# Unequal token blocks, ten attention phases and a new prologue order in a gated-attention and two-layer MLP kernel

## The chip, the cores and the metric

One NeuronCore of a Trainium2 chip runs the whole program. The time is device microseconds of one execution; the kernel before was run three times, and its median is what the kernel after is held against.

## What is computed

A gated linear attention over 768 positions for 4 batches of 8 heads of width 48 gives 3072 tokens of 384 features. Two dense layers follow.

```python
for t in range(S):
    state = f[:, :, t, :, None] * state + np.einsum('bhd,bhe->bhde', k[:, :, t], v[:, :, t])
    y[:, :, t] = np.einsum('bhd,bhde->bhe', q[:, :, t], state)
...
a = x @ w_a          # x: (3072, 384), w_a and w_b: (384, 1536)
b = x @ w_b
x = (a * b) @ w_out  # (1536, 384)
...
h = x @ w_in         # (384, 2048)
out = (h - np.tanh(h)) @ w_out2
```

The inputs are float32 (weights arrive as 64-bit numbers, whose bits VectorE turns into float32). Every dense product is made as three matmuls, high part by high, high by low and low by high (`mm_split`, L163 to L165), each operand being split into two parts.

## The kernel before

The attention is cut into 24 steps (`attn_step`, L293), one for 64 positions of two batches, which give 128 tokens. A step is a generator; each `next` issues one phase. Its phases, by the letters that the change gives them: **F** the sigmoid of the gates (ACT, L303) and **P** the running product of the gates (DVE, L304); **R** the reverse scan (DVE, L307 to L312); **K** three products KH, RA and RB (DVE, L317 to L319); **S** the scores sc and the transposes pk on PE (L321 to L328) and **M** their masking and copies (ACT, and POOL for the steps under `PSEL`, DVE for the others, L329 to L339); **U** the state update uu (PE, then DVE or ACT, then POOL, L341 to L364); **Y** the output yy on PE (L366 to L374) and **E** its split into x high and low (ACT and DVE, L375 to L385); **D** DMAs that put rows of x in place (L387 to L393).

Six token blocks of four steps (512 tokens) go through layer 1 (`moe1`, L474). A block has 12 inner rounds m of three slots, one group of nine matmuls each: a, then b, then y of the round before (L452 to L454). So a block has 36 slots (`SLOTS`). One PSUM bank holds a and one holds b, so b of the next round waits until gf = a*b (DVE, L494) has been made, and y waits for gh and gl, the two parts of gf.

The first four steps are the prologue, whose order is written out by hand as a string (`SEQ`, L58): a digit issues the next phase of that step, f, t, v and w issue loads, x a dummy matmul on PE, c one weight conversion. The other 20 steps are spread over the slots by `OFF` (L55): a step takes nine slots, and its phases come at fixed slots in it, three slots early (`LEAD`). Block 0 thus carries the four steps that block 1 needs, and so on; the last block carries none.

The weights of layer 1 are 36 tiles. Each is converted by three DVE instructions (`w_start`, L125 to L127) and split by one ACT copy and one POOL subtraction (`w_finish`, L137 to L139). Four conversions are started in the prologue, and one in each slot of block 0 (L546). The 32 tiles of layer 2 are converted in blocks 1 to 4, two per nine slots (`CONV`), there with the subtraction on DVE as well, and stored to DRAM; the last block loads them back. Layer 2 then runs with 1728 matmuls of 512 columns.

Every engine works through its queue in the order in which the program issues, and so does SP with most of the DMAs.

Of the kernel before, what the change touches and what calls it, by code (L numbers as in the profile page):

```python
# [28 lines left out]
def tile_kernel(ctx: ExitStack, tc: tile.TileContext, q, k, v, f, w_a, w_b, w_out, w_in, w_out2, l_fkq, l_tv, l_v, l_w1, l_w2, out):  # L29
# [14 lines left out]
        w.bitcast(I32) for w in (w_a, w_b, w_out, w_in, w_out2, l_w1, l_w2))  # L44

    NSTEP = 2 * NC
    blocks = [4, 4, 4, 4, 4, 4]
    NBLK = len(blocks)
    first = [sum(blocks[:j]) for j in range(NBLK)]
    block_of = [j for j, n in enumerate(blocks) for _ in range(n)]  # L50
    PRO = blocks[0]
    SLOTS = 3 * MF
    STEP = SLOTS // 4
    LEAD = 3
    OFF = (0, 1, 3, 5, 7, 8, 9)  # L55
    CONV = (2, 6)
    PSEL = 2 * PRO
    SEQ = ("f0 f1 t0 t1 v0 f2 t2 v1 w f3 t3 w v2 w v3 w x x x x 0 0 x 1 0 x 0 1 x 1 x 1 2 x 0 2 0 x 2 2 1 x 1 3 3 x 3 c 3 2 "  # L58
           "x 2 c f4 t4 v4 3 x c 3 x 4 x 4 c")
    TW = 528  # L60

    const = ctx.enter_context(tc.tile_pool(name="const", bufs=1))
# [49 lines left out]
    def w_load(item):  # L112
        name, m = item
        st = stage.tile([128, 2 * DM], I32, tag="wst", name="wst", bufs=3)
        src = l_w1[m, :, "abo".index(name)] if name in "abo" else l_w2[m, :, "ip".index(name)]
        nc.sync.dma_start(out=st, in_=src)
        return name, m, st
# [12 lines left out]
    def w_finish(item):  # L130
        name, m, st, c = item
        if name in "abo":
            wt = wpool.tile([128, 2, DM], F32R, tag="w", name=f"w_{name}{m}")
            W[name, m] = (wt[:, 0], wt[:, 1])
        else:
            wt = st.bitcast(F32R).rearrange("p (h n) -> p h n", h=2)
        nc.scalar.activation(wt[:, 0], c, ACTF.Copy)  # L137
        eng = nc.gpsimd if name in "abo" else nc.vector
        eng.tensor_tensor(wt[:, 1], c, wt[:, 0].bitcast(F32), ALU.subtract)  # L139
        if name not in "abo":  # L140
            spilled.append((name, m, wt))
# [25 lines left out]
    with tc.manual_schedule(), ExitStack() as p1:  # L167
# [65 lines left out]
        def t_of(i):  # L233
            return T[i if i < min(PRO, 4) else i % 2]

        def tv_of(i):
            return TV[i if i < min(PRO, 4) else i % 2]

        def w_of(i):
            return work[i if i < PRO else 0]  # L240

        def load_t(i, sl):
            t = t_of(i)
            if i < PRO:
                nc.sync.dma_start(out=t[:, sl], in_=l_fkq[i, :, sl])
            else:
                for r0 in (0, 64):
                    nc.sync.dma_start(out=t[r0:r0 + D, sl], in_=l_fkq[i, r0:r0 + D, sl])

        def load_v(i):  # L250
            w = w_of(i)
            for ab, (vs, r0) in enumerate(((w.VS_A, 64), (w.VS_B, 0))):
                nc.sync.dma_start(out=vs[r0:r0 + 64], in_=l_v[i, ab])
            if i < PRO:
                load_tv(i)

        def load_tv(i):
            nc.sync.dma_start(out=tv_of(i), in_=l_tv[i])
# [29 lines left out]
        Y3 = {}  # L288

        def warm():  # L290
            nc.tensor.matmul(bank(7, "warm"), wdum[:, 0:128], wdum, start=True, stop=True)

        def attn_step(i):  # L293
            c, hb = divmod(i, 2)
            jb = block_of[i]
            si = i - first[jb]
# [29 lines left out]
            for j in range(NJ):  # L326
                nc.tensor.transpose(  # L327
                    pk[:, 128 * j:128 * (j + 1)], KH[:, 2 * j:2 * j + 2, :].rearrange("p u s -> p (u s)"), ident)  # L328
            for r_, rows in ((RA, slice(64, 128)), (RB, slice(0, 64))):  # L329
                if i < PSEL:  # L330
                    nc.scalar.activation(r_[rows], sc[rows], ACTF.Copy)
                    nc.gpsimd.affine_select(
                        out=r_[rows], in_=r_[rows], compare_op=ALU.is_ge, fill=0.0,
                        base=0, pattern=[[0, U], [1, CH]], channel_multiplier=-1,
                    )
                else:
                    m3 = mask.unsqueeze(1)
                    nc.vector.tensor_tensor(r_[rows], sc[rows], m3[rows].to_broadcast([64, U, CH]), ALU.mult)
# [29 lines left out]
            for u in range(U - 2 if direct else U):  # L368
                for r0, vs, rr, ab in ((0, VS_A, RA, 0), (64, VS_B, RB, 1)):
                    dst = yy[r0:r0 + 64, u]  # L370
                    nc.tensor.matmul(dst, vs[:, u], rr[:, u], start=True, stop=not direct)  # L371
                    if direct:
                        nc.tensor.matmul(dst, VX[i % 2][ab][:, u % 2, u // 2], rr[:, U - 2 + u % 2],
                                         start=False, stop=True)  # L374
            if si == 0:  # L375
                X[jb] = xp.tile([128, 2, KT, 4, 128], F32R, tag="x", name="x")
                if not direct:
                    Y3[jb] = xp.tile([128, 2, 4, 128], F32R, tag="y3", name="y3", bufs=1)
# [24 lines left out]
        def flag(pr):  # L403
            nc.tensor.transpose(pr[0:1, 0:128], ru, ident)
            nc.vector.tensor_reduce(r2, pr[0:1, 0:128], mybir.AxisListType.X, ALU.min)
            nc.vector.tensor_scalar(okf, r2, 0.5, None, ALU.is_ge)

        gens = {i: attn_step(i) for i in range(NSTEP)}
        pulses = [(STEP * (i - PRO) - LEAD + o, i, p) for i in range(PRO, NSTEP) for p, o in enumerate(OFF)]
        pulses.sort(key=lambda e: e[0])  # L410

        def pulse(i, p):
            if p == 0 and i + 1 < NSTEP:
                load_t(i + 1, slice(0, 3))
                load_tv(i + 1)
            next(gens[i], None)
            if p == 5 and i + 1 < NSTEP:
                load_v(i + 1)

        def w_order(m, nm):  # L420
# [7 lines left out]
        half = []  # L428

        def w_tick(upto):  # L430
            while nconv[0] < upto and (loaded or half):
                if loaded:
                    half.append(w_start(loaded.pop(0)))
                    w_fetch()
                if len(half) > 1 or not loaded:
                    w_finish(half.pop(0))
                nconv[0] += 1

        def w_fetch(n=3):
            while WQ and len(loaded) < (n if WQ[0][0] in "abo" else 1):  # L440
                loaded.append(w_load(WQ.pop(0)))
# [65 lines left out]

        for it in SEQ.split():
            if it == "c":
                w_tick(nconv[0] + 1)  # L510
            elif it == "w":
                w_fetch(len(loaded) + 1)
            elif it == "x":
                warm()
            elif it[0] == "f":
                load_t(int(it[1]), slice(0, 1))
            elif it[0] == "t":
                load_t(int(it[1]), slice(1, 3))
            elif it[0] == "v":
                load_v(int(it[1]))  # L520
                if int(it[1]) >= PRO:
                    load_tv(int(it[1]))
            elif int(it) < PRO:
                next(gens[int(it)], None)
            else:
                pulse(int(it), pulses.pop(0)[2])
        for i in range(PRO):
            next(gens[i], None)
        npro = nconv[0]
        rot.update(n=2, conv=2)  # L530
        NW1 = 3 * MF + 1
# [11 lines left out]
        for g, jb in enumerate(moe1(None)):  # L543
            slot = g % SLOTS
            if jb == 0:
                w_tick(min(NW1, npro + slot + 1))  # L546
            else:
                if g == SLOTS:
                    rot.update(n=3, conv=None)
                if spilled:  # L550
                    w_spill()
                if (g + LEAD) % STEP in CONV:
                    w_tick(min(nconv[0] + 1, NW2 + 1))
            while pulses and pulses[0][0] <= g:
                _, i, p = pulses.pop(0)
                pulse(i, p)
            if not pulses and not done:
                done = True
                nc.vector.tensor_reduce(r1, MINP, mybir.AxisListType.X, ALU.min)
                nc.vector.tensor_scalar(r1, r1, P_MIN, None, ALU.is_ge)  # L560
            if jb == NBLK - 1:
                if slot == 2:
                    x2first.append(load_x2(0))
                elif slot > 2 and fills and len(fills) > 2 * MF2 + 3 - slot:
                    w_fill(*fills.pop(0))
# [37 lines left out]
        for i in range(NO * MF2 + LAG):  # L603
            g = None
            if i < NO * MF2:
                o, m = divmod(i, MF2)
# [3 lines left out]
                w = W["i", m]  # L610
# [3 lines left out]
                g = gelm_small(ph, lambda tag: gp2.tile([128, 512], F32, tag=tag, name=tag), usum[:, i:i + 1])  # L614
# [188 lines left out]
```

## Time and profile before

| | |
|---|---|
| median of 3 runs | 1018.9 us (1016.21 to 1019.22) |
| profiled execution | 1014.46 us, its span 1012.8 us |
| PE busy | 964.6 us, 95% |
| DVE busy | 648.6 us, 64% |
| ACT busy | 459.8 us, 45% |
| mean granted TensorE clock | 0.982 of full speed |

A row of the busy times by stretch names the stretch (us from the start of the span), its length, and for PE, PEld (weight loads), DVE, ACT and POOL the busy us and in brackets the instructions; then the granted TensorE clock, the DMA engines' mean busy share and GB/s. The stretches in the rows below begin where the first matmul of a block begins: block 0 at 48.72, block 1 at 164.04, block 2 at 255.06, block 4 at 439.78, block 5 at 532.09, layer 2 at 608.52.

### The profile page before, as it was taken

Reading aid. Unit: us, or ns where it says so; the run is one execution under the profiler, and the core shown is the slowest. Engines: PE = TensorE matmul, PEld = TensorE weight load, DVE = VectorE, ACT = ScalarE, POOL = GpSimd, SP = SyncE. Lnnn points to the kernel's source line nnn. Section 1 sums busy time; section 2 is a strip of 40 time slices with the busy share of each in tenths; the row PEclk is TensorE's granted clock in tenths of the full one; section 3 lists DMA queues with packets and bytes.
Section 4 is the critical chain, followed back from the end, with each engine's and each line's share of the span. In section 5 each row is a group of like instructions: output and inputs, shape, how many; then the busy total and the mean of one; then the engine's idle time right before and its main releaser. Section 6 shows DMA issues by size and latency. Waiting matters only on the chain.

```text
span 1012.8 us, 15883 instructions
## 1 busy us (share of the span) xinstructions
PE 964.6 (95%) x6153; PEld 776.9 (77%) x6153; DVE 648.6 (64%) x1102; ACT 459.8 (45%) x893; POOL 95.3 (9%) x115
## 2 busy tenths in 40 slices
PE   5778889999999999999999999999999999999997
PEld 3556777788788778877888888888888888888885
DVE  6488886766677667666663228666666666666663
ACT  3334433333333233333332127666666666666663
POOL 5245552000000000000000000000000000000000
PEclk9789989999999999999999999999999999999999
DMA  8175665434653554364427653010110100200000
GB/s 244 44 185 157 179 166 141 132 105 120 193 129 111 136 168 118 110 177 120 116 62 285 197 157 125 1 63 31 33 61 1 63 32 1 94 1 1 32 1 35
DMA packets 41170, 104.52 MB, mean 103 GB/s; under 512 B 5600, under 2 KB 8672, under 8 KB 41088
## 3 DMA queue, kind: packets, MB, share of 16 engines
q1 hardware_dynamic: 40368, 102.45, 34.3%
q10 hardware_dynamic: 720, 0.98, 0.5%
q8 instruction: 50, 0.82, 0.3%
q14 instruction: 32, 0.26, 0.1%
HBM read 74.71 MB, written 26.74 MB: 100 GB/s over the span
## 4 chain that ended last, share of the span: by engine, by line
PE 83%; DVE 9%; DMA 2%; issue 2%; ACT 2%; SPq 1%; DVEq 0%; ACTq 0%
PE o L165 20%; PE h L165 20%; PE a L165 13%; PE b L165 12%; PE y L165 11%; PE yy L371 2%; PE sc L324 1%; PE pk L327 1%; PE sc L323 1%; PE uu L353 1%; DVE cv L126 1%; DMA xs<-ol 1%; DVE cv L125 1%; DVE RB L319 1%; DVE gf L494 1%
## 5 line engine op out<-in xcount | busy, mean ns | idle before, releaser
L165 PE MATMUL h<-x,w_i 128*128 128x512 f32 x864 | 213.0, 391 | 0.0
L165 PE MATMUL o<-gh,w_p 128*128 128x512 f32 x576 | 194.7, 393 | 0.0
L165 PEld LDWEIGHTS h<-x,w_i 128*128 128x128 f32 x864 | 162.2, 188 | 36.4
L165 PE MATMUL a<-x,w_a 128*128 128x512 f32 x648 | 168.0, 404 | 0.5 <-DVE x L385 0.5
L165 PE MATMUL b<-x,w_b 128*128 128x512 f32 x648 | 158.7, 389 | 0.0
L165 PE MATMUL y<-gh,w_o 128*128 128x512 f32 x432 | 148.5, 398 | 0.0
L165 PEld LDWEIGHTS a<-x,w_a 128*128 128x128 f32 x648 | 121.1, 192 | 27.5 <-DVE x L385 0.8
L165 PEld LDWEIGHTS b<-x,w_b 128*128 128x128 f32 x648 | 121.7, 188 | 25.6
L105 DVE SCALAR_TENSOR_TENSOR xu<-u,h 128x512 f32<-128x512 f32 x96 | 66.0, 687 | 111.6 <-ACT u L102 111.4
L165 PEld LDWEIGHTS o<-gh,w_p 128*128 128x128 f32 x576 | 108.2, 188 | 24.7 <-issue 0.2
L495 ACT ACTIVATE gh<-gf 128x512 fp32r<-128x512 f32 x72 | 45.5, 632 | 178.9 <-DVE gf L494 174.8
L102 ACT ACTIVATE u<-h 128x512 f32<-128x512 f32 x96 | 57.3, 597 | 132.8 <-PE h L165 132.1
L165 PE MATMUL o<-gl,w_p 128*128 128x512 f32 x288 | 113.1, 393 | 0.0
L165 PEld LDWEIGHTS y<-gh,w_o 128*128 128x128 f32 x432 | 81.1, 188 | 18.6
L489 ACT ACTIVATE asb<-a 128x512 f32<-128x512 f32 x72 | 43.1, 598 | 102.4 <-PE a L165 102.3
L494 DVE TENSOR_TENSOR gf<-asb,b 128x512 f32<-128x512 f32 x72 | 49.0, 680 | 60.2 <-PE b L165 59.6
L165 PE MATMUL y<-gl,w_o 128*128 128x512 f32 x216 | 84.9, 393 | 0.0
L106 DVE SCALAR_TENSOR_TENSOR v<-v,xu 128x512 f32<-128x512 f32 x96 | 66.5, 692 | 10.4 <-ACT v L103 0.5
L107 DVE SCALAR_TENSOR_TENSOR v<-v,v 128x512 f32<-128x512 f32 x96 | 66.5, 693 | 10.3 <-ACT gh L574 0.5
L103 ACT ACTIVATE v<-u,bias 128x512 f32<-128x512 f32 x96 | 69.6, 725 | 3.1
L104 ACT ACTIVATE v<-u,bias 128x512 f32<-128x512 f32 x96 | 68.1, 710 | 0.6 <-DVE gl L575 0.6
L575 DVE TENSOR_TENSOR gl<-v,gh 128x512 fp32r<-128x512 f32 x96 | 65.8, 685 | 0.2 <-ACT gh L574 0.2
(102 smaller groups left out, 1110.1 us busy)
## 6 DMA issues: line engine op xcount, KB each, us to landing
wst<-in_l_w_dram SPq DMA_DIRECT2D x68, 384.0 KB, 3.4
wsp<-wst SPq DMA_DIRECT2D x32, 384.0 KB, 2.3
T<-in_l_fkq_dram SPq DMA_DIRECT2D x38, 288.0 KB, 5.2
x<-xs SPq DMA_DIRECT2D x12, 768.0 KB, 5.8
w_i<-wsp SPq DMA_DIRECT2D x16, 384.0 KB, 3.5
w_p<-wsp SPq DMA_DIRECT2D x16, 384.0 KB, 3.5
TV<-in_l_tv_dram SPq DMA_DIRECT2D x24, 192.0 KB, 5.6
xs<-oh SPq DMA_DIRECT2D x18, 256.0 KB, 2.2
```

The lines of the kernel that those rows point to most:

```text
L102: nc.scalar.activation(u, h, ACTF.Square, accum_out=total)
L103: nc.scalar.activation(v1, u, ACTF.Square, bias=bias1)
L104: nc.scalar.activation(v2, u, ACTF.Square, bias=bias2)
L105: nc.vector.scalar_tensor_tensor(xu, u, Q4, h, ALU.mult, ALU.mult)
L106: nc.vector.scalar_tensor_tensor(v1, v1, Q_Y1, xu, ALU.add, ALU.mult)
L107: nc.vector.scalar_tensor_tensor(v2, v2, Q_Y2, v1, ALU.add, ALU.mult)
L165: nc.tensor.matmul(dst, l_, r_, start=(first and i == 0), stop=(last and i == 2))
L371: nc.tensor.matmul(dst, vs[:, u], rr[:, u], start=True, stop=not direct)
L489: nc.scalar.activation(asb, pb, ACTF.Copy)
L494: nc.vector.tensor_tensor(gf, asb, pab[1], ALU.mult)
L495: nc.scalar.activation(gh, gf, ACTF.Copy)
L575: nc.vector.tensor_tensor(gl, g, gh.bitcast(F32), ALU.subtract)
```

## The change

The blocks have 4, 3, 3, 3, 3, 4 and 4 steps: seven blocks, of which blocks 1 to 4 have 384 tokens. Their matmuls, copies and products have 384 columns where 512 stood. Block j carries the steps of block j+1, so blocks 0 to 3 carry three steps and blocks 4 and 5 four; the phases of a step are spread over 12 slots where there are three steps, over nine where there are four. A step has ten phases that can be issued singly (two more places where the generator pauses, and M and E apart from S and Y). The prologue's string names each phase and each load; two conversions are started in it (both finished), where four were (three finished). The 32 tiles of layer 2 are spread as 7, 7, 7, 3 and 8 over blocks 1 to 5. `PSEL` becomes 7.

```diff
-    blocks = [4, 4, 4, 4, 4, 4]
+    blocks = [4, 3, 3, 3, 3, 4, 4]
...
-    STEP = SLOTS // 4
     LEAD = 3
-    OFF = (0, 1, 3, 5, 7, 8, 9)
-    CONV = (2, 6)
-    PSEL = 2 * PRO
...
+    PHASES = "FPRKSMUYED"
+    OFF = (0, 0, 1, 3, 5, 5, 7, 8, 8, 9)
+    NSPILL = (0, 7, 7, 7, 3, 8)
+    PSEL = first[2]
+    SEQ = ("lf0 lk0 lf1 lt0 lk1 lv0 lf2 lt1 lv1 lk2 w lf3 lt2 lv2 lk3 w lt3 lv3 w x x x x F0 P0 F1 R0 K0 x x x S0 P1 M0 F2 R1 K1 "
+           "U0 Y0 x S1 P2 M1 E0 F3 R2 K2 x U1 Y1 x S2 P3 M2 E1 R3 K3 x U2 Y2 x S3 c M3 E2 c lf4 lk4 lt4 lv4 U3 x Y3 e x E3 F4 P4")
...
             nc.scalar.activation(w.F3[:, :, 1:SL], tf.rearrange("p (u s) -> p u s", s=CH), ACTF.Sigmoid)
+            yield
             nc.vector.tensor_tensor_scan(w.PRE, w.F[:, 0:NS], D1, 0.0, ALU.mult, ALU.add)
...
-        pulses = [(STEP * (i - PRO) - LEAD + o, i, p) for i in range(PRO, NSTEP) for p, o in enumerate(OFF)]
+        pulses = []
+        for jb in range(1, NBLK):
+            for si in range(blocks[jb]):
+                for p, o in enumerate(OFF):
+                    at = (9 * si + o) * SLOTS // (9 * blocks[jb]) - LEAD
+                    pulses.append((SLOTS * (jb - 1) + at, first[jb] + si, p))
...
-                if (g + LEAD) % STEP in CONV:
+                nsp = NSPILL[jb] if jb < len(NSPILL) else 0
+                if (slot + 1) * nsp // SLOTS > slot * nsp // SLOTS or (jb == NBLK - 1 and slot == 0):
                     w_tick(min(nconv[0] + 1, NW2 + 1))
```

What moves in the queues is shown at two places. On DVE in the prologue, from the scan of step 1 to the scores' operands of step 2 (PRE is P, PM to R is phase R, KH to RB is K, x is E of step 0), before:

```order
L318 TENSOR_TENSOR RA<-T_187,PRE 64x512
L319 TENSOR_TENSOR RB<-T_187,PRE 64x512
L304 SCALAR_TENSOR_TENSOR PRE<-F,D_68 128x520
L307 TENSOR_SCALAR PM<-PRE 128x8
L308 RECIPROCAL D_135<-PM 128x8
L309 TENSOR_TENSOR MINP<-MINP,PRE 128x8
L310 SCALAR_TENSOR_TENSOR R<-F,D_135 128x520
L385 TENSOR_TENSOR x<-yy,x 128x3x128
L317 TENSOR_TENSOR KH<-xt,R 128x512
```

and in the kernel after:

```order
L317 TENSOR_TENSOR RA<-T_187,PRE 64x512
L318 TENSOR_TENSOR RB<-T_187,PRE 64x512
L303 SCALAR_TENSOR_TENSOR PRE<-F,D_68 128x520
L386 TENSOR_TENSOR x<-yy,x 128x3x128
L306 TENSOR_SCALAR PM<-PRE 128x8
L307 RECIPROCAL D_135<-PM 128x8
L308 TENSOR_TENSOR MINP<-MINP,PRE 128x8
L309 SCALAR_TENSOR_TENSOR R<-F,D_135 128x520
L316 TENSOR_TENSOR KH<-xt,R 128x512
```

E of step 0 has moved ahead of R of step 2.

On DVE in block 1, third step, where phase K comes (wc and wst are the conversion of a layer 2 tile, gf and gl those of layer 1), after the change:

```order
L504 TENSOR_TENSOR gf<-asb,b 128x384
L125 TENSOR_SCALAR wc<-wst 128x384
L126 SCALAR_TENSOR_TENSOR wc<-wst,wc 128x384
L127 SCALAR_TENSOR_TENSOR wc<-wst,wc 128x384
L139 TENSOR_TENSOR wst<-wc,wst 128x384
L316 TENSOR_TENSOR KH<-T_187,R 128x512
L317 TENSOR_TENSOR RA<-T_187,PRE 64x512
L318 TENSOR_TENSOR RB<-T_187,PRE 64x512
L511 TENSOR_TENSOR gl<-gf,gh 128x384
```

Before, the conversion and K stand in the same succession, but behind gl and ahead of gf:

```order
L501 TENSOR_TENSOR gl<-gf,gh 128x512
L125 TENSOR_SCALAR wc<-wst 128x384
L126 SCALAR_TENSOR_TENSOR wc<-wst,wc 128x384
L127 SCALAR_TENSOR_TENSOR wc<-wst,wc 128x384
L139 TENSOR_TENSOR wst<-wc,wst 128x384
L317 TENSOR_TENSOR KH<-T_185,R 128x512
L318 TENSOR_TENSOR RA<-T_185,PRE 64x512
L319 TENSOR_TENSOR RB<-T_185,PRE 64x512
L494 TENSOR_TENSOR gf<-asb,b 128x512
```

K has moved from the slot of a to the slot of b, and now waits for gf, so for the group b.

## Rows read from the trace of the kernel before

**Rows 1.** The page, part 1: busy us, share, instructions.

```profile
PE 964.6 (95%) x6153; PEld 776.9 (77%) x6153; DVE 648.6 (64%) x1102; ACT 459.8 (45%) x893; POOL 95.3 (9%) x115
```

**Rows 2.** Busy times by stretch: prologue, block 0, block 4, block 5, layer 2.

```profile
0.00:48.72 48.72, 31.56 (x481) 22.47 (x481) 28.54 (x62) 17.57 (x39) 20.41 (x41) 0.86 0.49 138
48.72:164.04 115.32, 97.84 (x716) 78.42 (x716) 93.19 (x164) 46.04 (x90) 59.48 (x58) 0.91 0.63 166
...
439.78:532.09 92.31, 90.32 (x725) 72.38 (x724) 62.73 (x119) 31.56 (x60) 3.38 (x4) 1.00 0.42 118
532.09:608.52 76.43, 76.43 (x334) 62.43 (x333) 19.72 (x30) 17.30 (x29) 0.00 (x0) 1.00 0.64 212
608.52:1012.80 404.28, 397.82 (x1730) 324.30 (x1728) 258.62 (x391) 254.29 (x500) 0.00 (x0) 1.00 0.10 36
```

**Rows 3.** Busy times by stretch: two whole steps (nine slots each) of block 0.

```profile
73.10:101.35 28.25, 24.26 (x183) 19.58 (x181) 24.54 (x42) 11.75 (x23) 14.86 (x16) 0.94 0.60 164
101.35:128.74 27.39, 24.13 (x183) 19.53 (x181) 23.72 (x42) 11.75 (x23) 15.86 (x16) 0.94 0.66 168
```

**Rows 4.** Waits in block 0: engine, line, waited for, us in total, times, longest.

```profile
PE sc L323 <- DVE RA L318: 15.2, 4, 6.2
...
DVE gf L494 <- PE b L165: 7.3, 4, 2.7
```

**Rows 5.** Groups on DVE, 73.10 to 128.74: busy us, mean ns, idle before.

```profile
L126 DVE SCALAR_TENSOR_TENSOR cv<-wst,cv 128x384 int32<-128x384 int32 x18 | 10.1, 561 | 0.6
L127 DVE SCALAR_TENSOR_TENSOR wc<-wst,cv 128x384 int32<-128x384 int32 x18 | 10.0, 554 | 1.9
L125 DVE TENSOR_SCALAR cv<-wst 128x384 int32<-128x384 int32 x18 | 9.9, 552 | 0.2
L494 DVE TENSOR_TENSOR gf<-asb,b 128x512 f32<-128x512 f32 x6 | 4.1, 677 | 2.5 <-PE b L165 2.4
```

**Rows 6.** Chain of waits in the prologue: start us, us, what.

```profile
18.47 1.25 DVE PRE L304
...
24.38 0.27 PE sc L324
...
30.12 0.50 ACT x L384
...
32.44 0.18 DVE PM L307
...
36.28 0.37 PE sc L324
...
40.87 0.41 PE yy L371 x2
...
44.23 0.50 ACT x L384
```

**Rows 7.** ACT in the prologue, timeline: the last of three copies of phase M, step 2.

```profile
27.18 0.58 ACT L339 ACTIVATE KTS<-pk 128x512 f32<-128x512 f32 x1
```

**Rows 8.** Busy times by stretch: first and second step of block 2.

```profile
255.06:280.42 25.36, 23.36 (x183) 18.53 (x182) 18.33 (x37) 9.46 (x19) 0.84 (x1) 1.00 0.68 187
280.42:302.74 22.32, 22.32 (x183) 17.94 (x181) 15.13 (x29) 7.40 (x15) 0.84 (x1) 1.00 0.44 119
```

**Rows 9.** Chain of waits in block 2: 32 matmuls of 48 columns.

```profile
292.56 0.61 PE uu L353 x32
```

**Rows 10.** Groups of weight loads: busy us, mean ns, idle before.

```profile
L165 PEld LDWEIGHTS a<-x,w_a 128*128 128x128 f32 x648 | 121.1, 192 | 27.5 <-DVE x L385 0.8 <-ACT x L384 0.5
...
L353 PEld LDWEIGHTS uu<-TV,KTS 64*64 64x64 f32 x768 | 15.4, 144 | 11.6 <-issue 10.1 <-ACT asb L489 1.1 <-ACT RA L331 0.3
```

**Rows 11.** DVE in block 2, in order of time: a conversion, K, gf.

```profile
257.96 0.35 DVE L125 TENSOR_SCALAR wc<-wst 128x384 int32<-128x384 int32 x1
...
259.89 0.68 DVE L317 TENSOR_TENSOR KH<-T,R 128x512 f32<-128x512 f32 x1
...
261.92 0.69 DVE L494 TENSOR_TENSOR gf<-asb,b 128x512 f32<-128x512 f32 x1
```

More of the change, by code (lines that the diff above doesn't have):

```diff
@@ L52, in tile_kernel @@
     SLOTS = 3 * MF
-    STEP = SLOTS // 4
     LEAD = 3
-    OFF = (0, 1, 3, 5, 7, 8, 9)
-    CONV = (2, 6)
-    PSEL = 2 * PRO
-    SEQ = ("f0 f1 t0 t1 v0 f2 t2 v1 w f3 t3 w v2 w v3 w x x x x 0 0 x 1 0 x 0 1 x 1 x 1 2 x 0 2 0 x 2 2 1 x 1 3 3 x 3 c 3 2 "
-           "x 2 c f4 t4 v4 3 x c 3 x 4 x 4 c")
+    PHASES = "FPRKSMUYED"
[4 more added lines that the diff above has]
+           "U0 Y0 x S1 P2 M1 E0 F3 R2 K2 x U1 Y1 x S2 P3 M2 E1 R3 K3 x U2 Y2 x S3 c M3 E2 c lf4 lk4 lt4 lv4 U3 x Y3 e x E3 F4 P4")
     TW = 528
@@ L253, in load_v @@
                 nc.sync.dma_start(out=vs[r0:r0 + 64], in_=l_v[i, ab])
-            if i < PRO:
-                load_tv(i)
         def load_tv(i):
@@ L328, in attn_step @@
                     pk[:, 128 * j:128 * (j + 1)], KH[:, 2 * j:2 * j + 2, :].rearrange("p u s -> p (u s)"), ident)
+            yield
             for r_, rows in ((RA, slice(64, 128)), (RB, slice(0, 64))):
@@ L374, in attn_step @@
                                          start=False, stop=True)
+            yield
             if si == 0:
@@ L408, in tile_kernel @@
         gens = {i: attn_step(i) for i in range(NSTEP)}
-        pulses = [(STEP * (i - PRO) - LEAD + o, i, p) for i in range(PRO, NSTEP) for p, o in enumerate(OFF)]
+        pulses = []
[4 more added lines that the diff above has]
+                    pulses.append((SLOTS * (jb - 1) + at, first[jb] + si, p))
         pulses.sort(key=lambda e: e[0])
+        phase = [0] * NSTEP
         def pulse(i, p):
-            if p == 0 and i + 1 < NSTEP:
+            assert phase[i] == p
+            phase[i] += 1
+            if i >= PRO and p == 0 and i + 1 < NSTEP:
                 load_t(i + 1, slice(0, 3))
@@ L416, in pulse @@
             next(gens[i], None)
-            if p == 5 and i + 1 < NSTEP:
+            if i >= PRO and PHASES[p] == "Y" and i + 1 < NSTEP:
                 load_v(i + 1)
@@ L512, in tile_kernel @@
                 w_fetch(len(loaded) + 1)
+            elif it == "e":
+                w_finish(half.pop(0))
             elif it == "x":
                 warm()
[L515 to L524, printed above, removed]
-            else:
-                pulse(int(it), pulses.pop(0)[2])
+            elif it[0] == "l":
+                i = int(it[2])
+                if it[1] == "f":
+                    load_t(i, slice(0, 1))
+                elif it[1] == "k":
+                    load_t(i, slice(1, 3))
+                else:
+                    (load_tv if it[1] == "t" else load_v)(i)
+            else:
+                i, p = int(it[1]), PHASES.index(it[0])
+                if i >= PRO:
+                    pulses.pop(0)
+                pulse(i, p)
         for i in range(PRO):
-            next(gens[i], None)
+            pulse(i, len(PHASES) - 1)
         npro = nconv[0]
```

## The prediction

> **What bounds the kernel now.** I read the page's shares first, then the busy times cut at the block starts, then the waits and groups of the stretches that differ. PE is busy 95% of the span [rows 1], so an engine beside it can gain nothing on the whole; what can be gained lies where PE is not full. The cuts show where [rows 2]: in the prologue PE is busy 31.56 of 48.72 us, in block 0 97.84 of 115.32 at a granted clock of 0.91, and from block 1 on almost always, at 1.00. Block 0 is the only long stretch in which DVE is nearly full, 93.19 us of 115.32. Two of its steps show the pattern [rows 3]: DVE is busy 24.54 of 28.25 and 23.72 of 27.39 us, mean 24.13 of 27.82, so 3.69 idle. PE meanwhile waits for phase K, 15.2 us in four waits, and DVE for a b group, 7.3 us in four [rows 4]. Block 0 is DVE's, with a wait passed to and fro; the later blocks and layer 2 are PE's.
>
> Prices for the later blocks: block 5 without any attention takes 76.43 us for 37 groups of nine matmuls (its own 36 and the last y of block 4) [rows 2], so 2.066 us a group, 229.5 ns a matmul. A step of attention adds 22.32 - 9 x 2.066 = 3.73 us, and the first step of a block 25.36 - 22.32 = 3.04 more, when the block before is stored [rows 8]. Three times 22.32 and 25.36 make the 92.3 of a block.
>
> **The prologue.** Between the scores of step 2 (24.38) and of step 3 (36.28) lie 11.90 us [rows 6]. In the old order PE did uu and yy of step 1 in that loop, and ACT could copy x only at 30.12. Now uu and yy of step 1 go ahead of the scores of step 2, and the loop is: scores and M's three copies, which end at 27.18 + 0.58 [rows 7], 3.4 after the scores begin; x on ACT and DVE, 30.12 to 31.20 [rows 6], 1.1; R and K, 32.44 to 36.28, 3.84; with 0.3 for signals 8.6 us, 3.3 less. But E now stands ahead of R on DVE where P alone had stood late (18.47), and x of step 0 has to wait for M of step 1 on ACT; I put the scores of step 2 at 25.0, 0.6 later than now. So the scores of step 3 begin at 33.6. From there to the first a is 12.44 us today, of which yy of step 2 took 40.87 to 44.23 [rows 6]; it goes ahead of the scores, leaving 9.1, and I take 9.4. The first a then begins at **43.0** instead of 48.72. The ends: 48.7, if the wait for x eats it all, and 41, if yy of step 2 runs at the higher of its two clocks, 2.4 GHz. The new order of loads I cost at nothing: every load of the prologue but that for step 4 is issued well before its use; if T of step 2 came late, DVE would wait for it directly.
>
> **Block 0.** It has three steps for 36 slots, 12 slots each, and two conversions less done ahead. Per step DVE gets three conversions (0.561 + 0.554 + 0.552 = 1.667 each) and one gf of 0.677 more [rows 5]: 24.13 + 5.00 + 0.68 = 29.8 us busy. PE needs 12 x 2.066 + 3.73 = 28.5, less, so DVE stays the bound. I leave its idle time at 3.7, since it waits for b at the same phases: 33.5 a step, 100.5 for three. Today's block is 115.32 - 4 x 27.82 = 4.0 longer than its steps, at its start; S of the first step now comes one slot later, and I take 2.0, between 0 and 4. Block 1 begins at 43.0 + 102.5 = 145.5, not 164.04: **18.5 saved**. The smaller lead of the weights counts: the split of a tile (one ACT copy, one POOL subtraction) is issued two slots before PE uses the tile, where it was four; that makes PE wait, and costs only where DVE then waits for b. Its ends are nothing and 2 us a step.
>
> **Blocks 1 to 4, 384 columns.** 972 matmuls of 512 columns become 1296 of 384. No row shows 384. Below, cost goes with columns: 172.1 ns. Above, a part is paid per matmul: 32 matmuls of 48 columns with their weight loads take 0.61 us [rows 9], 19 ns each, so at most 19 of the 229.5 are fixed, which gives 19 + 0.75 x 210.5 = 176.9. I take 177, the careful end: 1.593 a group, 57.3 for 36, against 55.8 in proportion, so 6.2 us for four blocks. The Trainium skill has a rule here, TensorE: Matmul & The Clock Gate, section Back-to-back issue gap: N/2.4 + 2.5 ns, 215.8 for 512 columns, where the trace has 229.5; by it 324 added matmuls would cost 0.8 us instead of 6.2, and the sum below would be 1007.5.
>
> On DVE the instructions that shrink (gf, gl, asb on ACT) are hidden under PE. What is not hidden: in the third step K comes after gf and a conversion. A conversion takes 257.96 to 259.89, K 259.89 to 261.92 [rows 11]; with 0.5 for gf that is 4.5 after the end of b, and PE has only y and a, 3.2, before S needs K: 1.3 lost. In the second step gl stands behind the rest of P, gf, the conversion and R; with P 1.25 [rows 6] and R 1.8 (3.84 less K) I estimate 5.7 us after the end of b, against 4.8 of the three groups until y needs gl: 0.9 lost. The store at the block's start costs 3.04 today because S sits in slot 2 behind a late K; S now sits in slot 3, and I take 1.0 (ends 0 and 3.0). A block of three steps: 57.3 + 3 x 3.73 + 2.2 + 1.0 = 71.7, three of them 215.1. Block 4, with four steps and three conversions, none between K and S: 57.3 + 14.9 + 1.0 = 73.2. More store DMAs (a block can cross a 512-token tile) lie on SP, whose transfers are awaited only in layer 2; past them wait loads of the next step, needed slots later.
>
> **The rest.** Block 5 has the width, steps and eight conversions of today's block 4: 92.3. Block 6 is today's block 5: 76.4. Layer 2 is unchanged: 404.3. From the start of block 1: 215.1 + 73.2 + 92.3 + 76.4 + 404.3 = 861.3, today 1012.8 - 164.0 = 848.8: **12.5 lost**, 8.1 of it in PE's work (one more step, 3.73, outside block 0) and narrower matmuls.
>
> **Sum.** -18.5 + 12.5 = -6.0 us: a span of 1006.8, an execution of 1008.5 against 1014.46. The median of the runs, 1018.9, lies 0.4% above the profiled one; taken from it, **1013**. About 0.3%, 3.1 us, is what a measurement of this kernel can tell from no change: faster is under 1015.8, slower over 1022.0.
>
> **Rivals.** *The short blocks become DVE's* (slower). The slots shrink by a quarter, DVE's work per step does not; where K or gl comes late in every step, not in the few counted, PE waits as in block 0. For it: the first step of a block already loses 3.04. Against it: in the other steps PE has no gap, 22.32 of 22.32, with DVE busy 15.13 [rows 8]. At 1.0 us more in ten of the 13 steps the time is 1023; it decides from 0.7 us a step in all 13. Chance 0.15.
>
> *The weight load sets the pace* of a narrow matmul. It is recorded with 192 ns, more than 177 [rows 10]; at 192 the 1296 matmuls cost 19 us more: 1032. Against it: the loads of uu are recorded with 144 ns while a matmul goes through every 19, so the recorded length is no floor [rows 9, 10]. Chance 0.06.
>
> *The head gains little*: the new order moves the waits and does not shorten them. First a at 45, and with the small lead of the weights 35.5 a step: block 1 at 153.5, 10.5 saved, 1021. For it: E ahead of R on DVE, and two conversions less before block 0. Chance 0.17.
>
> *Block 0 comes closer to DVE's busy time*: 1.0 idle a step, since the phases lie further apart; 8.1 less, 1005. Against it: DVE still waits for b after each S. Chance 0.12.
>
> *A narrow matmul costs in proportion*, 172.1 ns: 6.2 less, 1007. The page named above says nearly this. Against it: something of 229.5 is surely paid per matmul. Chance 0.10.
>
> The forecast keeps 0.40, with 1008 to 1018 as its own range.
>
> **The numbers.** Faster: 0.34 of the forecast, and the last two rivals, 0.56. Slower: 0.12 of the first rival, the second, and 0.02 of the third, 0.20. The same: 0.24. The range of 1001 to 1026 leaves out the second rival, the far end of the first, and the case that both last rivals hold, together some 0.15 to 0.2.
>
> **What would show it.** The first a near 43 and the first a of block 1 near 145; steps of block 0 near 33.5 with DVE busy near 30; groups of 384 columns at 1.59 us; blocks 1 to 3 at 71 to 72, with gaps of PE at S of the third step. The forecast is wrong if matmuls of 384 columns follow each other by over 182 ns, if block 1 begins after 150, or if blocks 1 to 3 take over 74.

## The result and the profile after

The changed kernel takes **1030.7 us** (1030.33 to 1031.27, four runs) where the kernel before takes 1017.9 (1016.21 to 1019.22, four runs): ratio 1.0127, 95% interval 1.0108 to 1.0145. It is slower, and outside the range that was given. The profiled execution has a span of 1028.5 us at a granted clock of 0.983, where 1006.8 had been worked out: 21.7 us to explain.

Busy times of the changed kernel by stretch (columns as in [rows 2]): prologue, blocks 0 to 4, layer 2.

```profile
0.00:40.42 40.42, 28.26 (x478) 20.19 (x478) 28.00 (x60) 17.23 (x39) 20.75 (x41) 0.96 0.57 167
40.42:155.26 114.84, 94.95 (x616) 68.80 (x616) 91.00 (x153) 41.03 (x81) 58.39 (x54) 0.93 0.58 157
155.26:227.62 72.36, 69.47 (x624) 65.19 (x625) 48.15 (x94) 25.06 (x52) 4.77 (x5) 1.00 0.48 137
227.62:302.14 74.52, 70.38 (x625) 66.51 (x625) 49.33 (x98) 24.67 (x52) 2.54 (x3) 0.98 0.49 137
302.14:376.49 74.35, 70.41 (x626) 66.53 (x625) 49.31 (x98) 24.68 (x52) 2.54 (x3) 0.98 0.51 138
376.49:454.24 77.75, 73.80 (x725) 68.98 (x725) 49.83 (x95) 26.21 (x54) 3.59 (x4) 0.98 0.40 102
...
623.01:1028.50 405.49, 397.81 (x1730) 324.56 (x1728) 258.39 (x391) 254.18 (x500) 0.00 (x0) 0.99 0.10 36
```

| term | forecast, us | measured, us | difference |
|---|---|---|---|
| prologue, to the first a | 43.0 | 40.4 | -2.6 |
| block 0 | 102.5 | 114.8 | +12.3 |
| blocks 1 to 3 | 215.1 | 221.2 | +6.1 |
| block 4 | 73.2 | 77.75 | +4.55 |
| blocks 5 and 6, layer 2 | 573.0 | 574.3 | +1.3 |

The loss sits in block 0 and in blocks 1 to 4. Two patterns show in the rows.

**Block 0.** The waits there (columns as in [rows 4]):

```profile
PEld a L165 <- POOL w_a L139: 15.8, 11, 2.1
PEld a L165 <- ACT w_a L137: 11.4, 8, 6.7
PE a L165 <- POOL w_a L139: 10.5, 8, 1.6
DVE gf L504 <- PE b L165: 10.2, 6, 1.7
PE a L165 <- ACT w_a L137: 8.1, 3, 6.3
```

In [rows 4] PE waited for phase K, and weights do not appear. Now PE waits for the two halves of the split of w_a, before nearly every a group (PE and PEld are one engine's matmuls and loads, so their waits overlap and are not added). The longest of these waits, 6.3 us, stands at the start of the block, before the second a group: the copy of its weights stands on ACT behind F of step 4, which waits for a DMA, and behind gh.

```profile
44.66 0.63 ACT L301 ACTIVATE F<-T 128x512 f32<-128x512 f32 x1 [4.29 <-DMA T<-in_l_fkq_dram]
...
50.96 0.51 ACT L137 ACTIVATE w_a<-wc 128x384 fp32r<-128x384 f32 x1
...
51.52 1.22 PE L165 MATMUL a<-x,w_a 128*128 128x512 f32 x2 [6.31 <-ACT w_a L137]
```

From the first a to the first S (57.15) go 16.7 us; then come two whole steps, and 23.6 us to the end of the block:

```profile
57.15:94.26 37.11, 32.01 (x209) 23.16 (x208) 31.00 (x52) 14.08 (x28) 20.97 (x19) 0.96 0.56 157
94.26:131.66 37.40, 32.17 (x209) 23.28 (x208) 31.21 (x53) 14.20 (x28) 20.94 (x19) 0.96 0.57 155
```

At the end of a step DVE, ACT, POOL and PE work as follows (start us, us, engine, line, instruction; the bracket is the idle time before it and what ended it):

```profile
87.07 0.68 DVE L504 TENSOR_TENSOR gf<-asb,b 128x512 f32<-128x512 f32 x1
...
87.84 0.63 ACT L505 ACTIVATE gh<-gf 128x512 fp32r<-128x512 f32 x1 [1.98 <-DVE gf L504]
...
88.38 0.51 ACT L137 ACTIVATE w_a<-wc 128x384 fp32r<-128x384 f32 x1
...
89.39 0.99 DVE L316 TENSOR_TENSOR KH<-T,R 128x512 f32<-128x512 f32 x1
...
89.79 1.45 POOL L139 TENSOR_TENSOR w_a<-wc,w_a 128x384 fp32r<-128x384 f32 x1
90.31 1.47 DVE L317 TENSOR_TENSOR RA<-T,PRE 64x512 f32<-64x512 f32 x1
91.20 1.45 POOL L139 TENSOR_TENSOR w_b<-wc,w_b 128x384 fp32r<-128x384 f32 x1
91.30 3.04 PE L165 MATMUL a<-x,w_a 128*128 128x512 f32 x7 [1.62 <-POOL w_a L139]
91.82 1.38 DVE L318 TENSOR_TENSOR RB<-T,PRE 64x512 f32<-64x512 f32 x1
```

Three things stand in these rows. The copy of w_a stands on ACT right behind gh, which waits for gf; so the weights of the next a are tied to the b group of this round. K stands on DVE behind gf and a whole conversion. And K's three instructions take 0.99 + 1.47 + 1.38 = 3.84 us while POOL subtracts; in [rows 11] KH took 0.68.

**Blocks 2 to 4.** Their first a group waits for phase D's DMAs. In the list of waits of the whole span the first line below is new. Below it is the start of block 2 on ACT and PE: three matmuls, 1.54 us of waiting, three more, 0.98 of waiting, the last three.

```profile
PE a L165 <- DMA x<-y: 9.2, 9, 2.2
...
224.84 1.93 ACTq L392 DMA_DIRECT2D x<-y  x3
...
227.62 0.69 PE L165 MATMUL a<-x,w_a 128*128 128x384 f32 x3
229.85 0.76 PE L165 MATMUL a<-x,w_a 128*128 128x384 f32 x3 [1.54 <-DMA x<-y]
231.59 1.26 PE L165 MATMUL a<-x,w_a 128*128 128x384 f32 x3 [0.98 <-DMA x<-y]
```

**The narrow matmul** is no part of what goes over the forecast. Six plain groups of 384 columns, 54 matmuls, in block 2 (the row counts 55, since the last matmul before them reaches into the stretch):

```profile
273.43:282.81 9.38, 9.38 (x55) 9.38 (x55) 7.46 (x16) 2.75 (x6) 0.00 (x0) 1.00 0.86 216
```

9.38 / 54 = 173.7 ns a matmul, against the forecast's 177.

### The profile page after: what moved, and what is told of

It is laid out like the page before. It is cut to its first block, busy times and chain, and to the rows that moved or that the text cites. A ratio compares the mean times of both kernels' runs of the same rounds, so it can differ in the third digit from the quotient of the medians.

```text
span 1028.5 us, 16648 instructions
## 1 busy us (share of the span) xinstructions
PE 971.6 (94%) x6475; PEld 815.6 (79%) x6475; DVE 656.2 (64%) x1131; ACT 461.4 (45%) x918; POOL 97.1 (9%) x113
## 4 chain that ended last, share of the span: by engine, by line
PE 80%; DVE 7%; DMA 4%; issue 3%; ACT 2%; POOL 2%; SPq 1%; ACTq 0%; DVEq 0%; POOLq 0%
PE o L165 19%; PE h L165 19%; PE a L165 12%; PE b L165 11%; PE y L165 11%; DMA x<-y 2%; PE yy L371 2%; PE sc L322 2%; DVE gf L504 1%; PE uu L353 1%; PE pk L326 1%; POOL w_a L139 1%; POOL gl L508 1%; DMA TV<-in_l_tv_dram 1%; DVE R L309 1%
## 5 line engine op out<-in xcount | busy, mean ns | idle before, releaser
L165 PE MATMUL a<-x,w_a 128*128 128x384 f32 (+1 forms) x756 | 176.1, 373 | 28.5 <-POOL w_a L139 10.5
L165 PEld LDWEIGHTS a<-x,w_a 128*128 128x128 f32 x756 | 136.2, 192 | 53.2 <-POOL w_a L139 15.8
L165 PE MATMUL b<-x,w_b 128*128 128x384 f32 (+1 forms) x756 | 167.0, 365 | 0.0
L165 PE MATMUL y<-gh,w_o 128*128 128x384 f32 (+1 forms) x504 | 157.7, 367 | 0.2
L165 PEld LDWEIGHTS b<-x,w_b 128*128 128x128 f32 x756 | 137.3, 191 | 13.1
L505 ACT ACTIVATE gh<-gf 128x384 fp32r<-128x384 f32 (+1 forms) x84 | 47.9, 571 | 172.4 <-DVE gf L504 168.0
L499 ACT ACTIVATE asb<-a 128x384 f32<-128x384 f32 (+1 forms) x84 | 45.1, 536 | 148.8 <-PE a L165 148.8
L504 DVE TENSOR_TENSOR gf<-asb,b 128x384 f32<-128x384 f32 (+1 forms) x84 | 50.7, 604 | 92.0 <-PE b L165 70.0
L165 PEld LDWEIGHTS y<-gh,w_o 128*128 128x128 f32 x504 | 94.0, 190 | 11.2 <-POOL w_o L139 1.7
L165 PE MATMUL y<-gl,w_o 128*128 128x384 f32 (+1 forms) x252 | 91.8, 364 | 1.5 <-DVE gl L511 1.5
L107 DVE SCALAR_TENSOR_TENSOR v<-v,v 128x512 f32<-128x512 f32 x96 | 66.5, 693 | 10.3 <-ACT gh L588 0.5
```

The source lines that it names most:

```text
L107: nc.vector.scalar_tensor_tensor(v2, v2, Q_Y2, v1, ALU.add, ALU.mult)
L165: nc.tensor.matmul(dst, l_, r_, start=(first and i == 0), stop=(last and i == 2))
L499: nc.scalar.activation(asb, pb, ACTF.Copy)
L504: nc.vector.tensor_tensor(gf, asb, pab[1], ALU.mult)
L505: nc.scalar.activation(gh, gf, ACTF.Copy)
```

## Experiments

All times are medians; each ratio is against the kernel before, run on the same chip. Block 0 and the sum of blocks 1 to 4 are cut at the first a of each block in the profiled execution. "Narrow" has the change's blocks, "old" six blocks of four steps; blocks 1 to 4 hold 1536 tokens in the one and 2048 in the other, so their sums compare only within a kind.

| run | blocks | us | ratio, 95% interval | block 0 | blocks 1 to 4 |
|---|---|---|---|---|---|
| before | old | 1017.9 | | 115.3 | 368.1 |
| the change | narrow | 1030.7 | 1.0108 to 1.0145 | 114.8 | 299.0 |
| four ahead | narrow | 1025.7 | 1.0054 to 1.0094 | 109.7 | 300.7 |
| three ahead | narrow | 1025.6 | 1.0047 to 1.0090 | 108.8 | 300.9 |
| D earlier | narrow | 1017.5 | 0.9993 to 1.0012 | 114.6 | 286.1 |
| parts close | narrow | 1016.3 | 0.9982 to 1.0002 | 109.3 | 290.1 |
| parts close, four ahead | narrow | 1009.2 | 0.9904 to 0.9937 | 105.4 | 288.8 |
| K earlier, four ahead | narrow | 1009.6 | 0.9927 to 0.9965 | 99.4 | 292.5 |
| K and D earlier | narrow | 1022.2 | 1.0042 to 1.0073 | 122.1 | 283.4 |
| K and D earlier, four ahead | narrow | 998.8 | 0.9811 to 0.9846 | 98.4 | 282.5 |
| prologue alone | old | 1003.4 | 0.9848 to 0.9881 | 111.7 | 365.5 |
| prologue, three ahead | old | 1003.2 | 0.9846 to 0.9886 | 114.4 | 364.4 |
| prologue, four ahead | old | 1002.9 | 0.9827 to 0.9871 | 116.1 | 363.9 |
| prologue, four ahead, K earlier | old | 999.1 | 0.9816 to 0.9847 | 111.2 | 364.1 |
| prologue, S and U later | old | 1026.8 | 1.0092 to 1.0126 | 138.5 | 367.3 |
| prologue, S and U later, four ahead | old | 1012.9 | 0.9967 to 0.9999 | 121.7 | 366.0 |

### The lead of the weights

First theory: with two conversions ahead, the split of w_a comes too late. Rivals: the wait for the gates of step 4 at the start, and the spreading of three steps over 36 slots.

```diff
-           "U0 Y0 x S1 P2 M1 E0 F3 R2 K2 x U1 Y1 x S2 P3 M2 E1 R3 K3 x U2 Y2 x S3 c M3 E2 c lf4 lk4 lt4 lv4 U3 x Y3 e x E3 F4 P4")
+           "U0 Y0 x S1 P2 M1 E0 F3 R2 K2 x U1 Y1 x S2 P3 M2 E1 R3 K3 x U2 Y2 x S3 c M3 E2 c lf4 lk4 lt4 lv4 U3 x Y3 e x E3 c c F4 P4")
```

Four ahead (above):

> The changed kernel with four conversions started before block 0 instead of two (two more behind E of step 3); nothing else. Lead theory: in the changed kernel the split of the next a tile is queued on ACT right behind gh and on POOL right behind gl of the group before, so nearly every a group of block 0 waits 1.5 to 2 us; with four ahead it is issued two slots earlier, the a groups go back to 2.1 us, the step period of block 0 from 37.2 to about 34, block 0 from 114.8 to 103 to 106, the run from 1030.7 to about 1020. Startup rival (the loss is T of step 4, for which ACT waits 4.3 us, and the late first step): the period stays at 37, block 0 at 110 to 115, the run above 1026. Spreading rival (three steps on 36 slots, in ten parts, fill DVE): the period stays at 37, the run at 1030.

Three ahead (one c in place of two):

> The changed kernel with three conversions started before block 0 instead of two. Lead theory in its queue form (what counts is that the ACT copy stands ahead of gh, not how many slots ahead): most of the gain is there with three, a period of about 34.5, block 0 near 106, the run near 1022. If the lead counts slot by slot: half the gain, a period of 35.5, block 0 near 109, the run near 1025. Startup and spreading rivals: no change, 1030.

They came to 1025.7 and 1025.6: 5 us of the loss, half of what the theory asked for. That three do as much as four speaks for the queue: what counts is that the copy of w_a stands ahead of gh. But the step period fell only from 37.1 and 37.4 to 36.5 and 35.4 us. The a groups no longer wait, and the time went back to the old wait. Waits in block 0 with four ahead:

```profile
PE sc L322 <- DVE RA L317: 14.4, 3, 6.3
...
DVE gf L504 <- PE b L165: 7.9, 6, 2.7
```

PE waits at S for K, three times (four times in [rows 4], where the block has four steps). The lead was one limit lying over another.

### The prologue with the old blocks

```diff
-    blocks = [4, 3, 3, 3, 3, 4, 4]
+    blocks = [4, 4, 4, 4, 4, 4]
...
-    NSPILL = (0, 7, 7, 7, 3, 8)
+    NSPILL = (0, 8, 8, 8, 8)
```

Two conversions ahead:

> The prologue of the changed kernel (two conversions ahead, ten parts) with the blocks of the kernel before: six blocks of four steps, eight conversions for layer 2 in each of blocks 1 to 4. Lead theory: block 0 loses here as well, 9 to 13 us beside the 115.3 of before, which takes back the 8.3 that the first a gains; the run comes to 1019 to 1023. Spreading rival (it is the three steps in block 0): block 0 stays near 115.3 and the run comes to about 1009.6.

Four ahead (with the diff of the section before):

> The same as the prologue alone (blocks of four steps), with four conversions started before block 0. Lead theory: first a at 40.4 to 42, block 0 at 115 to 116, all later blocks as before, the run 6 to 8 us under the kernel before, 1010 to 1012. Rival (block 0 is DVE's, so that what the prologue saves comes back in it as waiting for DVE): block 0 at 120 or more and the run within 3 us of the kernel before.

Three ahead:

> The new prologue and ten parts with blocks of four steps, three conversions ahead instead of two or four. With two ahead PE waits for a tile a little in most groups, with four it waits long at S, and both came to 1003. If the two waits only trade places: 1002 to 1004 again. If each is an avoidable loss: 1000 to 1001.

All three came to 1003, 14 us faster than the kernel before; the first two had been expected at 1009.6 or more. My theory on the lead was refuted here: with steps of nine slots, two ahead cost nothing, and the waits only trade places (block 0 is 111.7, 114.4 and 116.1). So the prologue and the ten phases are worth 14 us (these kernels also keep the change's spreading of the conversions for layer 2, in which every other one comes one slot later than before; its share is not separated), and the narrow blocks, as the change makes them, cost 27. The 6.5 to 8 us of the earlier first a are not all of the 14: block 0 with two ahead is 3.7 shorter than before, and blocks 1 to 4 are 2.6 shorter together.

### D earlier

```diff
-    OFF = (0, 0, 1, 3, 5, 5, 7, 8, 8, 9)
+    OFF = (0, 0, 1, 3, 5, 5, 7, 8, 8, 8.5)
...
-                    at = (9 * si + o) * SLOTS // (9 * blocks[jb]) - LEAD
+                    at = int((9 * si + o) * SLOTS // (9 * blocks[jb])) - LEAD
```

> The changed kernel with part D (the copies of y's rows into x) issued one slot earlier in each block; nothing else. Lead-of-D theory: blocks 2 to 4 begin with an a group that waits for D's transfers (3.5 to 5.0 us instead of 1.6), because D's lead is three slots as before while a slot shrank from 2.07 to 1.56 us; one slot more gives back 2 to 2.5 us in each of blocks 2, 3 and 4, and the run comes to 1023 to 1026. Rival (the transfers are late because DVE and ACT reach the last step's E late, or because D's issue on ACT holds up F of the next step): the blocks keep 74.4 and the run stays within 1.5 us of 1030.7.

The run fell by 13.2 us to 1017.5, twice what the theory asked for. Blocks 1, 2 and 4 of this run:

```profile
156.88:227.40 70.52, 68.91 (x626) 65.19 (x625) 49.32 (x95) 24.72 (x52) 4.80 (x5) 1.00 0.51 145
227.40:297.63 70.23, 68.62 (x625) 65.20 (x625) 49.16 (x98) 24.41 (x52) 2.54 (x3) 1.00 0.52 146
...
368.22:443.02 74.80, 72.17 (x725) 67.95 (x725) 48.41 (x94) 26.11 (x54) 3.60 (x4) 1.00 0.41 105
```

PE no longer waits for x<-y anywhere. Against the change, blocks 1 to 4 are 1.8, 4.3, 3.8 and 2.9 us shorter, 12.8 together, where PE's waits in the change are 1.9, 2.5, 2.3 and 2.5. What blocks 2 and 3 gain beyond the wait goes with the clock. In block 2 of the change PE was busy 2.50 of the 5.03 us of the first a group; then the granted clock fell, and b ran at 0.55 of full speed, mostly at the lower level of 1.2 GHz, and took 2.67 us for 1.56:

```profile
227.62:232.65 5.03, 2.50 (x10) 1.92 (x10) 4.93 (x10) 0.94 (x2) 0.00 (x0) 0.90 0.91 202
232.65:235.32 2.67, 2.67 (x10) 2.67 (x10) 0.61 (x2) 0.49 (x1) 0.00 (x0) 0.55 0.37 147
```

With D earlier the granted clock is 1.00 in all four blocks. The issue on ACT still takes 1.9 us, and asb waits for it in four blocks, 10.3 us in all; that costs nothing visible.

### The parts of a step close together

```diff
-                    at = (9 * si + o) * SLOTS // (9 * blocks[jb]) - LEAD
+                    at = si * SLOTS // blocks[jb] + o - LEAD
```

Two ahead:

> The changed kernel with the parts of a step no longer stretched over 12 slots: offsets counted in slots, as in the kernel before, each step beginning every 12 slots; two conversions ahead. Place-of-K theory: stretched, K stands on DVE behind gf and a conversion, beside a subtraction on POOL, and its three instructions take 3.83 us instead of 2.05, and S on PE waits; close together, K stands ahead of gf again, takes 2.05 us, and the step period of block 0 falls from 37.2 to 34 to 35; D also comes three slots earlier, which gives back 2 to 2.5 us in each of blocks 2 to 4: the run comes to 1014 to 1019. Lead theory (two conversions ahead are the limit): the period stays over 36, the run over 1020. Rival that three steps in a block as such cost it: nothing changes, 1030.

Four ahead:

> As the run with the parts close together, with four conversions ahead of block 0. If place of K and lead both count: period 33.5, block 0 at 102 to 104 as predicted, the run 1011 to 1015. If only the place counts: the same as with two ahead.

K is back ahead of gf and, but for one KH of 1.44 us, undisturbed. With two ahead the period stayed at 37.5 and 36.5 us, as the lead theory said, though the time lies in the other theory's range; with four it fell to 34.7 and 34.8 (33.5 expected), block 0 to 105.4 (102 to 104 expected). Both lose less in blocks 1 to 4, where D comes three slots earlier. The edit moves every part, so it does not tell which one counts.

### K alone

With four ahead, and of the stretched parts only K one slot earlier:

```diff
-    OFF = (0, 0, 1, 3, 5, 5, 7, 8, 8, 9)
+    OFF = (0, 0, 1, 2.25, 5, 5, 7, 8, 8, 9)
...
-                    at = (9 * si + o) * SLOTS // (9 * blocks[jb]) - LEAD
+                    at = int((9 * si + o) * SLOTS // (9 * blocks[jb])) - LEAD
```

> The changed kernel with four conversions ahead, and of the stretched parts K alone one slot earlier, ahead of gf (in blocks of three steps as in those of four). Against the run with four ahead alone (period 35.9, block 0 at 109.7, 1025.7 us). Theory (beside a subtraction of POOL that reads SBUF, K's three instructions take 3.83 us instead of 2.05): K takes 2.05, the period falls by 1 to 1.8, block 0 by 3 to 5.4; the later blocks keep 74.5 where D waits; the run 1020 to 1022.5. Rival (the stretch as such, not K's neighbours): K takes 2.05, but the period stays above 35.5 and the run above 1024.

16 us less than with four ahead alone, three times the expectation or more. The period is 32.8 us, 3.1 less; K takes 2.05 us, which is 1.8 of it, and the rest is put down to S, which no longer waits for gf and a conversion (PE's wait for K in block 0 fell from 14.4 to 5.2 us). Block 0 is 99.4. In blocks 1 to 3 the stall of S in the third step, 0.77 and 0.33 us in each, is gone as well. They are 2.1, 3.6 and 2.9 us shorter, more than the stall: in blocks 2 and 3 the granted clock is 1.00 where it was 0.98, and PE is busy 68.4 and 68.5 us for 70.2 and 70.3. Why the clock held, with a wait of PE for D still there, is not shown.

### All three, and without the lead

K and D earlier and four ahead (K at 2.25 and D at 8.5, and the diff of the lead):

> The changed kernel with all three repairs: four conversions ahead, K one slot earlier, D one slot earlier. If they are separate causes that add up: block 0 at 99 to 101, blocks 1 to 3 at 70 to 71, block 4 at 74 to 75, the run 1002 to 1004, as fast as the new prologue with the old blocks. If they share a cause: no better than the run with four ahead and K earlier, 1006 to 1010.

K and D earlier, two ahead:

> K and D each one slot earlier, but two conversions ahead as in the change. If the lead costs by itself: block 0 at 104 to 106, the run 1007 to 1010. If only K's place cost in block 0: 99 to 101, 1002 to 1004. If with two ahead the weights of a are the limit whatever K does: block 0 at 112 to 115, the run 1015 to 1018.

With all three the run is 998.8 us, 1.7% under the kernel before: below the expectation, and the lowest of the table. Its block 0, two whole steps of it, block 1 and layer 2, then K in the second step of block 0:

```profile
42.12:140.50 98.38, 88.31 (x615) 70.66 (x616) 88.31 (x159) 41.93 (x83) 55.55 (x55) 0.97 0.69 183
...
51.99:84.86 32.87, 31.89 (x208) 25.69 (x209) 29.32 (x53) 14.12 (x28) 20.20 (x19) 0.90 0.68 183
84.86:117.66 32.80, 29.06 (x209) 23.32 (x209) 30.22 (x53) 14.12 (x28) 19.21 (x19) 1.00 0.65 177
...
140.50:209.47 68.97, 68.46 (x625) 64.92 (x624) 47.31 (x89) 23.91 (x50) 4.41 (x4) 1.00 0.50 138
...
592.01:997.10 405.09, 397.80 (x1730) 324.31 (x1728) 258.53 (x391) 254.51 (x500) 0.00 (x0) 1.00 0.10 36
...
83.44 0.69 DVE L316 TENSOR_TENSOR KH<-T,R 128x512 f32<-128x512 f32 x1
84.04 0.68 DVE L317 TENSOR_TENSOR RA<-T,PRE 64x512 f32<-64x512 f32 x1
84.75 0.69 DVE L318 TENSOR_TENSOR RB<-T,PRE 64x512 f32<-64x512 f32 x1
```

The first S comes at 52.0, 9.9 us after the first a, although F of step 4 begins at 45.4 here and at 44.7 in the change: the late load of step 4 does not by itself make the loss at the start of block 0.

Without the lead the same kernel takes 1022.2, outside all three expectations: block 0 is 122.1, longer than in the change. The repairs do not add up. Its second step:

```profile
92.09 0.69 DVE L504 TENSOR_TENSOR gf<-asb,b 128x512 f32<-128x512 f32 x1
...
92.87 0.63 ACT L505 ACTIVATE gh<-gf 128x512 fp32r<-128x512 f32 x1 [4.02 <-DVE gf L504]
...
93.41 0.51 ACT L137 ACTIVATE w_a<-wc 128x384 fp32r<-128x384 f32 x1
...
93.97 0.89 PE L165 MATMUL a<-x,w_a 128*128 128x512 f32 x2 [2.07 <-ACT w_a L137]
...
95.87 3.35 PE L165 MATMUL a<-x,w_a 128*128 128x512 f32 x7 [1.01 <-POOL w_a L139]
...
99.15 0.37 PE L322 MATMUL sc<-RA,KH 64*64 64x64 f32 x1
...
103.94 0.69 DVE L504 TENSOR_TENSOR gf<-asb,b 128x512 f32<-128x512 f32 x1 [5.73 <-PE b L165]
```

K now stands ahead of gf. So gf is late, and through gh and the copy of w_a the a group too; S stands behind that a on PE, b behind S, and the next gf waits 5.73 us for b. (By the loop of the change, S of a block's step si comes in slot 12 si + 3 where a block has three steps and in slot 9 si + 2 where it has four: behind an a group in the first, ahead of one in the second.) It is a ring through four queues, which four ahead cut at w_a: 23.4 us with K earlier, 5 with K late. Of the 23.7 us in block 0, 9.3 are lost before the first S, which comes 19.2 us after the first a; there F of step 4, which waits for its load, stands in the ring too. No run loads step 4 earlier, so its share is not separated.

### S and U later, with the old blocks

```diff
-    OFF = (0, 0, 1, 3, 5, 5, 7, 8, 8, 9)
+    OFF = (0, 0, 1, 3, 6, 6, 8, 8, 8, 9)
```

Two ahead:

> The new prologue with blocks of four steps and two conversions ahead, S and M one slot later, U one slot later and Y in the slot of U. In the first step of blocks 1 to 4 the scores wait 0.6 us and uu 1.3 us for work queued behind the store of the block before; the stretched blocks, with one more group between, hardly pay it. Theory: 1.5 to 2 us less in each of four blocks, 995 to 998 instead of 1003.4. Rival: the wait moves to yy or to D, which now comes right behind E: 1002 to 1006.

Four ahead:

> The same with four conversions ahead. In block 0 S is what PE waits for with four ahead (22 us in all); one slot later it waits less, but DVE waits for b after S as before. Theory: block 0 stays DVE's, 114 to 116, the later blocks gain as with two ahead: 995 to 998. If S's wait is what sets block 0: 111 to 113, 992 to 995.

Both runs missed their expectations: 1026.8 and 1012.9 us. Block 0 grew by 27 and 6 us, and blocks 1 to 4 gained nothing. Waits in block 0 of the first:

```profile
DVE gf L504 <- PE b L165: 22.7, 4, 5.8
PEld a L165 <- ACT w_a L137: 20.4, 7, 8.9
...
PE yy L371 <- DVE T L361: 8.9, 4, 2.2
```

The first two lines are the ring of the section before, with S moved behind a by hand. The third is new: yy right behind uu waits for DVE's sum over uu.

### K earlier, with the old blocks

The old blocks with four ahead, and K in `OFF` from 3 to 2:

> The new prologue with blocks of four steps, four conversions ahead, K one slot earlier (behind y's group, right behind R). With four ahead S waits 22 us in all for K in block 0. If K's place sets that wait: block 0 from 116 to 111 to 113, the run 998 to 1000. Rival (K meets a subtraction on POOL there and takes 3.8 us instead of 2.05, or stands beside the later blocks' gl): block 0 at 115 or more, the run 1002 or more.

The run takes 999.1 us, and block 0 is 111.2, 4.8 less. K's place counts there too, although RB meets a subtraction of POOL and takes 1.37 us. This kernel and the repaired narrow one cannot be told apart (intervals 0.9816 to 0.9847 and 0.9811 to 0.9846).

## Why the prediction was wrong

**Prologue: right.** First a at 40.4 against 43.0. Scores of step 2 at 25.2 (25.0 expected), of step 3 at 32.9 (33.6); the last stretch took 7.6 us where I took 9.4. Kernels with this prologue begin between 40.4 and 42.4, and with it alone the kernel is 14 us faster. The rival by which the head gains little is refuted.

**Block 0: the step that failed.** "I leave its idle time at 3.7, since it waits for b at the same phases." It does not. Stretched over 12 slots, K moved behind gf and a conversion, as I had seen for block 1, and I priced that move only there. K then takes 3.84 us for 2.05, which makes DVE busy 31.1 us a step for the 29.8 of the sum, and idle time grew to 6.1. With K ahead and the lead restored, DVE is busy 29.3 and 30.2 us and idle about 3, in a period of 32.8: the sum of instructions was right, and their place made the difference. In the forecast's own reckoning, 11.2 of the 12.3 us over it are in the step (37.25 us for 33.5, three times) and 1.1 at the block's start (3.1 for 2.0). The second part of the same step, "the smaller lead of the weights", had the ends "nothing and 2 us a step". It costs 5 us in block 0 as the change stands, within those ends, and 24 once K is early, far outside them: the price of a lead depends on what else stands in the queue.

**Blocks 1 to 4: a wait that I did not list.** "The store at the block's start [...] I take 1.0" covers only S. D's lead was three slots before and after, but a slot shrank from 2.07 to 1.56 us, so the DMAs had 4.7 instead of 6.2 us. One slot more of lead takes 12.9 us off these blocks, the wait and what it did to the clock, more than the whole excess of 10.7 over the forecast of these blocks; with D one slot earlier they take 286.1 where 288.3 were forecast, block 4 1.6 over its 73.2 and blocks 1 to 3 3.8 under their 215.1. The price of K's place, "1.3 lost" in the third step, was near: S stalls 1.1 us there. The split of the loss is misadded: one more step, 3.73, and the narrower matmuls, 6.2, are 9.9 and not 8.1; nothing else rests on it. The rival that short blocks become DVE's named the wrong engine: DVE is busy 49 of 74 us there.

**Narrow matmuls: right, a little too dear.** 173.7 ns against 177, close to the proportional 172.1. By these rows the 1296 matmuls cost 1296 x 173.7 - 972 x 229.5 = 2.0 us more than the 972, not 6.2. The rival that the weight load sets the pace, 192 ns, is refuted. The Trainium skill's formula for a single matmul (TensorE: Matmul & The Clock Gate, section Back-to-back issue gap) gives an estimate of 162.5 ns for 384 columns; the rows have 173.7 and, for 512, 229.5, so its level does not hold here, though the 0.8 us that it gives for the added matmuls is nearer than my 6.2.

**Blocks 5 and 6 and layer 2** took 92.3, 76.4 and 405.5 us against 92.3, 76.4 and 404.3.

What stays open: why two ahead cost 2 us a step with the parts close together and nothing in the old blocks, where K and S have the same neighbours. In the old blocks the granted clock of block 0 is 0.97 with two ahead and 0.90 with four, with the parts close together 0.94 and 0.92; whether that decides it, no run shows.

## What to carry to other kernels

A lead counted in slots is a time: when slots get shorter, recount in microseconds the lead of every DMA that is hidden behind them. When a phase is moved, price what stands ahead of it and beside it on every engine in each stage where it runs, not in one; and look for rings through in-order queues (here gf, gh, w_a, a, S, b), because a repair at one place of a ring can cost time until the other is made. A change that bundles a gain and a loss should be timed in its parts: the new prologue alone was 14 us faster, and three small moves brought the narrow blocks from 27 us behind the old ones to level with them.

## What the runs showed of the hardware

K's products take up to twice as long on DVE beside a subtraction on POOL, 1.47 us for 0.68 in RA, and POOL's subtraction grows from 1.02 to 1.45. Without POOL beside it RA takes 0.67 to 0.68 us in the steps of blocks 1 to 4. In the rows of block 0 above they seem to take turns: RA begins at 90.31 and ends 0.54 after w_a's subtraction (91.24), the subtraction of w_b ends 0.87 after RA (91.78), RB 0.55 after w_b (92.65). The Trainium skill (SBUF — State Buffer, section Who interferes with whom) has the rule: a VectorE instruction with two inputs in SBUF contends with a GpSimd instruction that reads SBUF, and the one that starts second is blocked. These rows agree; so does the conversion, whose instructions in block 0 have one operand in SBUF (the other, cv, is in PSUM): they kept the 0.55 to 0.56 us of [rows 5] beside POOL's subtractions.

The granted clock can fall behind a short stall: after 5.03 us in which PE was busy 2.50, nine matmuls of 384 columns ran at a granted clock of 0.55 and took 2.67 us for 1.56 (block 2 of the change, section on D). In blocks 1 and 4, with 1.9 and 2.5 us of waiting, the groups behind the wait kept 1.00.
